# Moving operands of the fp32r matmuls read as two blocks in turn, with the storage orders set up in DRAM

## The chip, the cores and the metric

The kernel runs on one core of one Trainium2 chip. The metric is the device time of one execution in microseconds (us). Runs of this kernel agree within about 0.1%: three runs of the kernel before took 2607.55, 2608.79 and 2609.8 us.

## The reference

The input `x` is 8 batches of 3072 positions by 256 channels, in float32. Along the positions each channel is convolved with a filter given by its spectrum, and the result goes through a bilinear layer:

```
X = np.fft.rfft(x, axis=1)
F = (filt_r + 1j * filt_i)[None, :, :]
y = np.fft.irfft(X * F, n=3072, axis=1).astype(np.float32)
t = y.reshape(8 * 3072, 256)
out = ((t @ w_a) * (t @ w_b)) @ w_out          # w_a, w_b: 256 x 1536, w_out: 1536 x 256
```

## The kernel before

**The transform.** 3072 is factored as 128 x 24. A forward transform takes two steps of matmuls with tables of cosines and sines as weights: `s1` over the 128 (it takes one pair of the 24 residues at a time, 12 pairs a batch) and `s2` over the 24 (16 tiles a batch). The filter is multiplied in behind `s2` on VectorE, and the inverse goes back by `is1` (16 tiles) and `is2` (six groups `c` of four residues, in two halves `k`). Between the steps the data goes through DRAM (`zd`, `td`).

**The bilinear layer.** A visit `(c, p)` handles one group of 512 positions and one pair of 128-column blocks of `w_a` and `w_b`. It makes seven products by a 2 x 2 Strassen scheme (`product`, with the bank names x, y and z), multiplies the a part by the b part on VectorE (`parts`), splits the result into a high and a low part (`split`, on ScalarE and GpSimd), and projects it with `w_out` into the accumulators po0 and po1 (`project`). There are 36 visits a batch and 288 in all.

**The number format.** To be accurate in float32, nearly every matmul is made three times: high x high, low x high and high x low. The operands are then of the type fp32r (F32R in the code). A matmul has a stationary operand (its weights, 128 columns, loaded by one LDWEIGHTS before each matmul) and a moving operand, whose columns are streamed past the weights: 256 columns in `s1`, `product` and `project`, 512 in most of `s2` and `is1`. `is2` and the transform of batch 0 (the `first_` functions) use plain fp32 operands, except for 24 fp32r matmuls in `first_s1`.

**Which operand moves.** In `product` the moving operand is the activations `ah`/`al` (made in `is2`, 256 positions), in `project` it is a row block of `w_out` (256 output channels), in `s1` it is the input `xh`/`xl`, in `s2` the transformed data `zt`, and in `is1` the filtered spectrum `yh`/`yl` (256 channels each, one or two of them).

**What sets the order.** The order on each engine is written out by hand (`manual_schedule`). The visits are the main loop; `plan` and `early` put the steps of the next batch's transform into slots between the products of a visit: the pairs of `s1` in the first half of a batch, and one tile of `s2` and one of `is1` in each of 16 visits of the second half. SyncE (SP) issues nearly all loads, ScalarE's queue the stores of the transform.

**Names and lines.** L385 is the matmul of `s1`; L420, L422 and L423 those of `turn`, which `s2` and `is1` call (L420 for tile 0 alone); L615 that of `is2`; L646 that of `product`; L678 that of `project`; L537, L499, L501, L505 and L517 belong to batch 0's front. On VectorE, L657 is `parts`, L915, L935 and L937 add up the products, L433, L435 and L441 multiply by the filter. `filts`, `nyq` hold the filter's rows and its last row; `small_tables` issues four small loads at the start.

Of the kernel before, what the change touches and what calls it, by code (L numbers as in the profile page):

```python
# [9 lines left out]
F32 = mybir.dt.float32  # L10
# [4 lines left out]
ALU = mybir.AluOpType  # L15
# [3 lines left out]
B, S, D, DFF = 8, 3072, 256, 1536  # L19
N1, N2 = 128, 24  # L20
NB = 32
# [5 lines left out]
NJ = 16  # L27
ORDER = [(w[0], int(w[1])) for w in "a0 b0 a1 b1 o0 a2 b2 o1 o2 a3 b3 o3 a4 b4 a5 b5 o4 o5".split()]
EARLY = 11
BESIDE = {i: (11 + i, None) for i in range(7)}  # L30
ODD = [1, 5, 7, 11, 13, 17, 19, 23]

FOLDED = [0, 12] + [n for k in range(1, 12) for n in (k, 24 - k)]
WHOLE = [0, 3, 6, 9]
# [30 lines left out]
def _exact(v, n):  # L65

    if n in ODD or n % 6 == 0:
        return v
# [7 lines left out]
def _tables():  # L76
# [3 lines left out]
    g = np.zeros((N2, 128, N1))  # L80
    for n2 in range(N2):
        n = N2 * n1 + n2
        for j in range(NB):
            for s in range(2):
                k1 = 32 * s + j
                r, i = 4 * j + s, 4 * j + 2 + s
# [52 lines left out]
    order = [n for p in PAIRS for n in p]  # L139
    hi, lo = np.zeros((2, 96, 128)), np.zeros((2, 96, 128))  # L140
    bhi, blo = np.zeros((2, 128, 96)), np.zeros((2, 128, 96))
    fc = np.zeros((128, 3, 128))
    ic = np.zeros((128, 3, 96))
    fix = np.vectorize(_exact)
    for kind in range(2):
# [4 lines left out]
        for ri in range(2):  # L150
            for s in range(2):
# [3 lines left out]
                for k2 in range(N2):  # L155
                    r = 64 * ri + 24 * s + k2
                    row = inv[kind, r] * fac[k2]
                    bhi[kind, r], blo[kind, r] = _split(row if kind else fix(row, k2))
    fl = hi.transpose(1, 0, 2)
    fc.reshape(4, 32, 3, 128)[:, :24] = np.stack([hi[0], hi[1], lo[1]], 1).reshape(4, 24, 3, 128)  # L160
    ic[:, 0], ic[:, 1], ic[:, 2] = bhi[0], bhi[1], blo[1]
    sc = np.zeros((128, 2))
# [10 lines left out]

    s1c = np.stack(_split((s1 / fac[:, None, None])[order]), 1).reshape(NI, 2, 2, N1, 128).transpose(0, 3, 1, 2, 4)
    s1f = s1[[0, 12, *range(1, 12)]].transpose(1, 0, 2)
    g = g.reshape(N2, NJ, 2, 4, N1).transpose(0, 1, 3, 2, 4)
    gc = g.reshape(NC, 4, 128, N1).transpose(0, 2, 1, 3)
    ff, fi = fwd.reshape(2, 4, N2, 128)[:, :, FOLDED], np.zeros((128, 4, 96))
    ff[:, 2:, [f > 12 for f in FOLDED]] *= -1
    ff = ff.reshape(2, 96, 128).transpose(1, 0, 2)  # L180
# [25 lines left out]


@with_exitstack
def fft_filter_bilinear_kernel(ctx: ExitStack, tc, x, x0, filt, fny, wa, wb, wo, s1c, gc, fc, fl, ic, sc, s1f, ff, fi, out):
    nc = tc.nc  # L210
    f32 = lambda t: t.bitcast(F32)

    def pool(name, bufs=1, space=None):
        kw = {} if space is None else {"space": space}
# [8 lines left out]
    fr = front.enter_context(tc.tile_pool(name="fr", bufs=2, side="right"))  # L223
# [19 lines left out]
    def bank_f(shape, kind=F32, lane=0):  # L243
        if kind == F32 and not streaming:
            turns[0] += 1
        tag = f"f{lane}" if kind != F32 else "f1" if streaming else f"f{turns[0] % 2}"
        return ps_f.tile(shape, kind, name="ps", tag=tag)
# [16 lines left out]
    cut = pw.tile([128, 2], F32, name="cut")  # L264
    filts = [const.tile([128, 2, 2, D], F32, name=f"filt{i}") for i in range(2)]
    nyq = const.tile([128, D], F32, name="nyq")


    def conv_load(w, queue):
# [69 lines left out]
    for k, p in ORDER:  # L339
        if k == "o":  # L340
            conv.append([wo.bitcast(I32).rearrange("(f p) (d w) -> p f d w", p=128, w=2)[:, 2 * p:2 * p + 2], p, 2])
        else:
            w = (wa if k == "a" else wb).bitcast(I32).rearrange("(k p) (f w) -> p k f w", p=128, w=2)
# [36 lines left out]
    def s1(b, i):  # L380
        (xh, xl), st = held.pop(("xs", b, i)), held.pop(("s", b, i))
        ps = bank_f([128, 2, D])
        for n in range(2):
            for q, (w, m) in enumerate(((0, xh), (0, xl), (1, xh))):
                nc.tensor.matmul(ps[:, n], st[:, n, w], m[:, n], start=q == 0, stop=q == 2)  # L385
        zh = later[0].tile([128, 2, D], F32R, name="zh", tag="e1")
        zl = later[0].tile([128, 2, D], F32R, name="zl", tag="e2")
        nc.scalar.copy(out=zh, in_=ps)
        nc.vector.tensor_tensor(out=zl, in0=ps, in1=f32(zh), op=ALU.subtract)
        held["zs", b, i] = zh, zl  # L390
# [25 lines left out]
    def turn(i, w, wl, hi, lo, ps):  # L416

        if i == 0:
            for q, (m, v) in enumerate(((w[:, 1], hi), (wl[:, 1], lo), (w[:, 2], hi))):
                nc.tensor.matmul(ps[:, 0], m, v[:, 0], start=q == 0, stop=q == 2)  # L420
        j = 1 if i == 0 else 0
        nc.tensor.matmul(ps[:, j:2], w[:, 0], hi[:, j:2], start=True, stop=False)  # L422
        nc.tensor.matmul(ps[:, j:2], wl[:, 0], lo[:, j:2], start=False, stop=True)  # L423

    half = [slice(0, 64), slice(64, 128)]

# [93 lines left out]

    def first_f(g):
        f = [*filts, more][g % 3].rearrange("p a n d -> p (a n) d")
        nc.sync.dma_start(out=f, in_=filt[64:192, 4 * g:4 * g + 4])
        held["f0", g] = f

    def first_z(g, parts=1):
# [25 lines left out]
    def first_s2(i):  # L552
        g, h = divmod(i, 2)
        zt, f = (held[k, g][:, 2 * h:2 * h + 2] for k in ("z0", "f0"))
        bank, tag = BANKS[i % 4]
        ps = bank.tile([128, 2, D], F32, name="ps", tag=tag)
        first_turn(i, [fcf], [zt[0:96]], ps)
        y = fr.tile([128, 2, D], F32, name="y0", tag="y", bufs=4)
        v = fr.tile([128, 2, D], F32, name="v0", tag="v", bufs=4)

        nc.vector.tensor_tensor(out=y, in0=ps, in1=f, op=ALU.mult)
        if ("w", i) in held:
            nc.vector.tensor_tensor(out=v, in0=ps, in1=held.pop(("w", i)), op=ALU.mult)
        else:
            nc.vector.tensor_tensor(out=v[0:64], in0=ps[64:128], in1=f[0:64], op=ALU.mult)
            nc.vector.tensor_tensor(out=v[64:128], in0=ps[0:64], in1=f[64:128], op=ALU.mult)
        if i == 0:
            r = 64 if 0 in swapped else 0
            nc.vector.tensor_tensor(out=v[r:r + 1, 0], in0=ps[64:65, 0], in1=nyq[64:65], op=ALU.mult)
        held["y0", i] = [y, v]  # L570

    def first_is1(i):
# [37 lines left out]

    def is2(b, c, k):
        tt, gt, ah, al = held["t", b, c]
        ps = bank_f([128, 4, N1])
        for n in range(4):
            nc.tensor.matmul(ps[:, n], tt[:, n, 128 * k:128 * k + 128], gt[:, n], start=True, stop=True)  # L615
        ps = ps.rearrange("p (h n) m -> p h (n m)", h=2)
        v = nc.vector
        if k == 0:
            x0 = moe[0].tile([128, 2, 256], F32, name="x0", tag="x0")
            t = moe[0].tile([128, 4, 256], F32, name="t", tag="ot")  # L620
            held["b", b, c] = x0, t
            nc.scalar.copy(out=x0, in_=ps)
            nc.scalar.copy(out=ah[:, 0], in_=x0[:, 0])
            v.tensor_tensor(out=t[:, 0], in0=ps[:, 1], in1=x0[:, 0], op=ALU.subtract)
            v.tensor_tensor(out=al[:, 0], in0=x0[:, 0], in1=f32(ah[:, 0]), op=ALU.subtract)
            return
        x0, t = held.pop(("b", b, c))
        nc.scalar.copy(out=ah[:, 1:3], in_=ps)
        v.tensor_tensor(out=al[:, 1:3], in0=ps, in1=f32(ah[:, 1:3]), op=ALU.subtract)
        v.tensor_tensor(out=t[:, 1], in0=ps[:, 1], in1=t[:, 0], op=ALU.subtract)  # L630
        v.tensor_tensor(out=t[:, 2], in0=ps[:, 1], in1=x0[:, 1], op=ALU.subtract)
        v.tensor_tensor(out=t[:, 3], in0=ps[:, 0], in1=t[:, 1], op=ALU.subtract)
        for i in (0, 2):
            nc.scalar.copy(out=ah[:, 3 + i:5 + i], in_=t[:, i:i + 2])
            nc.gpsimd.tensor_tensor(out=al[:, 3 + i:5 + i], in0=t[:, i:i + 2], in1=f32(ah[:, 3 + i:5 + i]), op=ALU.subtract)
# [4 lines left out]
    def product(b, c, p, i, bank, first=False):  # L640
        m, n = FACTORS[i]
        _, _, ah, al = held["t", b, c]
        for k in range(2):
            wh, wl = wab[p][k]
            for q, (w, v) in enumerate(((wh, ah), (wh, al), (wl, ah))):
                nc.tensor.matmul(  # L646
                    bank[:, k], w[:, m], v[:, n], start=first and k == 0 and q == 0, stop=q == 2, skip_group_check=True
                )

# [20 lines left out]
    def project(r, f, some=range(4)):  # L670
        b, c, p = r["at"]
        gh, gl = (t.rearrange("p h (n m) -> p (h n) m", n=2) for t in r[f"f{f}"])
        if p == r["from"] and f == 0:
            po[b, c] = [ps_o.tile([128, 2, D], F32, name=f"po{i}", tag=f"po{i}") for i in range(2)]
        for n in some:
            o = po[b, c][n // 2][:, n % 2]
            for q, (g, w) in enumerate(((gh, wo_h), (gh, wo_l), (gl, wo_h))):
                nc.tensor.matmul(  # L678
                    o, g[:, n], w[p][:, 1 - f], start=p == r["from"] and f == 0 and n % 2 == 0 and q == 0,
                    stop=p == r["to"] and f == 1 and q == 2, skip_group_check=True,  # L680
                )
# [73 lines left out]
    with tc.manual_schedule():  # L755
# [29 lines left out]
        def small_tables():  # L785
            nc.sync.dma_start(out=fcf, in_=ff)
            nc.sync.dma_start(out=icf, in_=fi)
            nc.sync.dma_start(out=nyq[64:65], in_=fny)
            nc.sync.dma_start(out=sct, in_=sc)

# [54 lines left out]
        for b in range(B):  # L845
# [55 lines left out]
            for v, (c, p) in enumerate(VISITS if b == 0 else [(c, p) for c in range(NC) for p in range(NP)]):  # L901
# [3 lines left out]
                r = {"at": (b, c, p), "from": NP // 2 if halves and p >= NP // 2 else 0, "to": NP // 2 - 1 if halves and p < NP // 2 else NP - 1}  # L905
# [46 lines left out]
        one, r = prev  # L952
# [43 lines left out]
```

## Time and profile before

| what | value |
|---|---|
| median of three runs | 2608.79 us |
| the profiled execution | 2609.38 us |
| its span, first to last instruction | 2607.5 us |
| TensorE busy, matmul / weight load | 99% / 96% |
| VectorE, ScalarE, GpSimd busy | 70%, 54%, 48% |
| mean granted TensorE clock | 0.997 of full speed |
| matmuls, each with one weight load | 20934 |

How to read it: matmuls are pipelined, and the duration that the profile gives for one (about 280 ns for 256 columns) is the time from its start to its modelled end, so consecutive ones overlap. What a matmul costs in a full stream is its pitch: the difference of the start times of two neighbours. Pitches are read from the timeline, whose first column is the start in us. A line of the timeline that ends in x4 merges four equal instructions.

### The profile page before, as it was taken

To read this page: it belongs to the slowest core of one execution; us is meant where nothing else is said; L and a number is where in the kernel's file an instruction comes from. 1 tells how busy PE (TensorE), PEld (TensorE's weight loads), DVE (VectorE), ACT (ScalarE), POOL (GpSimd) and SP (SyncE) were. 2 spreads that over 40 slices of the span, in tenths; PEclk is the share of its full clock that TensorE was granted. 3 is DMA by queue.
4 is the path that set the end of the run, shared out by engine and by line. 5 is a ranking of instruction groups with operands and counts; after the bars stand their busy time and mean duration, and the time that the engine had idled before them with its cause. 6 is when DMAs were issued, how large, how long until landed. Compare 5 with 4: busy or idle time off the path is not lost.

```text
span 2607.5 us, 53389 instructions
## 1 busy us (share of the span) xinstructions
PE 2572.0 (99%) x20934; PEld 2508.2 (96%) x20934; DVE 1813.1 (70%) x2511; ACT 1409.5 (54%) x2480; POOL 1246.8 (48%) x926
## 2 busy tenths in 40 slices
PE   7899999999999999999999999999999999999999
PEld 3699999999999999999999999999999999999999
DVE  6776995569855797558965589655995569855554
ACT  5655555555555455555555555555555555544444
POOL 4664544445445454444444444444554445534333
PEclk9999999999999999999999999999999999999999
DMA  9446433344323552245413544144432444310100
GB/s 307 150 135 212 136 120 99 135 136 144 103 93 130 152 154 84 90 139 164 137 63 117 162 133 127 55 157 137 134 114 84 142 138 141 101 36 22 41 21 17
DMA packets 209421, 310.65 MB, mean 119 GB/s; under 512 B 19185, under 2 KB 119474, under 8 KB 209090
## 3 DMA queue, kind: packets, MB, share of 16 engines
q1 hardware_dynamic: 166578, 230.55, 28.6%
q10 hardware_dynamic: 42592, 76.70, 8.4%
q8 instruction: 164, 2.69, 0.4%
q14 instruction: 87, 0.71, 0.1%
HBM read 202.31 MB, written 108.45 MB: 119 GB/s over the span
## 4 chain that ended last, share of the span: by engine, by line
PE 94%; DMA 2%; POOL 1%; DVE 1%; issue 1%; ACT 1%; SPq 0%; ACTq 0%; DVEq 0%; POOLq 0%
PE x L646 31%; PE po L678 31%; PE z L646 15%; PE y L646 8%; PE ps L615 3%; PE ps L385 2%; PE ps L422 2%; PE ps L423 2%; DMA filt<-in_filt 1%; DMA z<-x 0%; PE ps L420 0%; DMA zf<-z 0%; POOL m L316 0%; DMA td<-t 0%; DMA gt<-in_gc 0%
## 5 line engine op out<-in xcount | busy, mean ns | idle before, releaser
L666 POOL TENSOR_TENSOR gl<-g,gh 128x512 fp32r<-128x512 f32 x574 | 785.4, 1370 | 898.6 <-ACT gh L665 884.7
L657 DVE TENSOR_TENSOR g<-c 128x512 f32<-128x512 f32 x576 | 598.8, 1040 | 292.1 <-ACT c L946 171.5
L678 PE MATMUL po<-woh,gh 128*128 128x256 f32 x2304 | 655.1, 284 | 2.2 <-DVE filt L685 2.2
L678 PE MATMUL po<-woh,gl 128*128 128x256 f32 x2304 | 646.6, 281 | 0.0
L678 PE MATMUL po<-wol,gh 128*128 128x256 f32 x2304 | 645.2, 280 | 0.0
L946 ACT COPY c<-x 128x512 f32<-128x512 f32 x288 | 169.0, 587 | 780.1 <-PE x L646 753.2
L678 PEld LDWEIGHTS po<-woh,gh 128*128 128x128 f32 x2304 | 434.7, 189 | 12.8 <-DVE filt L685 2.6
L678 PEld LDWEIGHTS po<-wol,gh 128*128 128x128 f32 x2304 | 434.5, 189 | 7.5
L678 PEld LDWEIGHTS po<-woh,gl 128*128 128x128 f32 x2304 | 433.9, 188 | 0.1
L665 ACT CAST gh<-g 128x512 fp32r<-128x512 f32 x576 | 357.3, 620 | 63.0 <-PE po L678 52.8
L935 DVE TENSOR_TENSOR c<-x,c 128x512 f32<-128x512 f32 x288 | 197.7, 686 | 219.0 <-PE x L646 196.2
L646 PE MATMUL x<-ah,wah 128*128 128x256 f32 x1152 | 325.5, 283 | 4.5 <-ACT c L910 3.2
L646 PE MATMUL x<-ah,wbl 128*128 128x256 f32 x1152 | 323.4, 281 | 0.0
L646 PE MATMUL x<-al,wbh 128*128 128x256 f32 x1152 | 323.1, 280 | 0.0
L646 PE MATMUL x<-al,wah 128*128 128x256 f32 x1152 | 322.9, 280 | 0.0
L646 PE MATMUL x<-ah,wbh 128*128 128x256 f32 x1152 | 322.6, 280 | 0.0
L646 PE MATMUL x<-ah,wal 128*128 128x256 f32 x1152 | 322.0, 280 | 0.0
L646 PEld LDWEIGHTS x<-ah,wah 128*128 128x128 f32 x1152 | 217.6, 189 | 5.9 <-ACT c L910 4.0
L646 PEld LDWEIGHTS x<-al,wah 128*128 128x128 f32 x1152 | 218.4, 190 | 0.0
L646 PEld LDWEIGHTS x<-ah,wal 128*128 128x128 f32 x1152 | 217.6, 189 | 0.0
L646 PEld LDWEIGHTS x<-ah,wbl 128*128 128x128 f32 x1152 | 217.0, 188 | 0.0
L646 PEld LDWEIGHTS x<-ah,wbh 128*128 128x128 f32 x1152 | 216.9, 188 | 0.0
(145 smaller groups left out, 5950.5 us busy)
## 6 DMA issues: line engine op xcount, KB each, us to landing
z<-zh ACTq DMA_DIRECT2D x112, 256.0 KB, 2.3
filt<-in_filt SPq DMA_DIRECT2D x112, 256.0 KB, 2.8
zth<-z SPq DMA_DIRECT2D x112, 256.0 KB, 3.0
tt<-td SPq DMA_DIRECT2D x94, 256.0 KB, 4.0
out<-ot SPq DMA_DIRECT2D x47, 512.0 KB, 3.0
td<-t ACTq DMA_DIRECT2D x114, 192.0 KB, 2.1
xt<-in_x SPq DMA_DIRECT2D x84, 256.0 KB, 3.5
st<-s1d SPq DMA_DIRECT2D x84, 256.0 KB, 2.7
```

The costliest lines, as they stand in the source:

```text
L385: nc.tensor.matmul(ps[:, n], st[:, n, w], m[:, n], start=q == 0, stop=q == 2)
L422: nc.tensor.matmul(ps[:, j:2], w[:, 0], hi[:, j:2], start=True, stop=False)
L423: nc.tensor.matmul(ps[:, j:2], wl[:, 0], lo[:, j:2], start=False, stop=True)
L615: nc.tensor.matmul(ps[:, n], tt[:, n, 128 * k:128 * k + 128], gt[:, n], start=True, stop=True)
L646: nc.tensor.matmul(bank[:, k], w[:, m], v[:, n], start=first and k == 0 and q == 0, stop=q == 2, skip_group_check=True)
L657: nc.vector.tensor_tensor(out=gt, in0=g[:, :, 0], in1=g[:, :, 1], op=ALU.mult)
L665: nc.scalar.copy(out=gh, in_=gt)
L666: low.tensor_tensor(out=gl, in0=gt, in1=f32(gh), op=ALU.subtract)
L678: nc.tensor.matmul(o, g[:, n], w[p][:, 1 - f], start=p == r["from"] and f == 0 and n % 2 == 0 and q == 0, stop=p == r["to"] and f == 1 and ...
L935: nc.vector.tensor_tensor(out=c1[:, 1], in0=bx, in1=c1[:, 1], op=ALU.add)
L946: nc.scalar.copy(out=c1[:, 0], in_=bx)
```

## The change

No instruction changes its place on any engine, and one small DMA on SP is added. What changes is the access pattern of the operands and the order in which data is stored:

- A helper `mm` takes the moving operand of `s1`, `product`, `project` and of tile 0 in `turn` as two blocks of 128 columns, and reads them in turn: column 0 of the first block, column 0 of the second, column 1 of the first, and so on. The output is written in one run as before. The other matmuls of `turn` do the same for 2 x 256 columns. With the pattern written as pairs of step and count, a moving operand was [1, 256] and is [1, 128] [128, 2].
- So that the output columns come out in their natural order, the stored operand has the even columns first and the odd ones behind. `_halves` makes that order. `w_out` and the filter are given to the kernel in that order (`FILTERED`), and `x` in the order that becomes natural after three such reads (`GIVEN`): `s1`, `s2` and `is1` each undo one level.
- For `product` the table `g` of `is2` has its 128 columns in that order, and `is2` writes each matmul's output as two runs of 64 columns, so that `ah`/`al` stand with the even positions first.
- Batch 0's front is not changed and keeps the natural order; it gets its own copies of the filter in DRAM (`filt0`, `fny0`) and its own tile `nyq0` of 1 KB a partition, filled by one more DMA in `small_tables`.
- The 24 fp32r matmuls of `first_s1` (L505) read one run as before.

```diff
+def _halves(order):
+    return np.asarray(order).reshape(-1, 2).T.ravel()
+FILTERED = _halves(range(D))
+TURNED = _halves(FILTERED)
+GIVEN = _halves(TURNED)
...
-    g = g.reshape(N2, NJ, 2, 4, N1).transpose(0, 1, 3, 2, 4)
+    g = g[:, :, _halves(range(N1))].reshape(N2, NJ, 2, 4, N1).transpose(0, 1, 3, 2, 4)
...
+    def mm(out, w, m, **kw):
+        out, m = out.rearrange("p (a k) -> p a k", k=2), m.rearrange("p (k a) -> p a k", k=2)
+        nc.tensor.matmul(out, w, m, **kw)
...
-                nc.tensor.matmul(ps[:, n], st[:, n, w], m[:, n], start=q == 0, stop=q == 2)
+                mm(ps[:, n], st[:, n, w], m[:, n], start=q == 0, stop=q == 2)
...
-        j = 1 if i == 0 else 0
-        nc.tensor.matmul(ps[:, j:2], w[:, 0], hi[:, j:2], start=True, stop=False)
-        nc.tensor.matmul(ps[:, j:2], wl[:, 0], lo[:, j:2], start=False, stop=True)
+                mm(ps[:, 0], m, v[:, 0], start=q == 0, stop=q == 2)
+            for q, (m, v) in enumerate(((w[:, 0], hi), (wl[:, 0], lo))):
+                mm(ps[:, 1], m, v[:, 1], start=q == 0, stop=q == 1)
+            return
+        out, hi, lo = ps.rearrange("p j (a k) -> p j a k", k=2), *(v.rearrange("p j (k a) -> p j a k", k=2) for v in (hi, lo))
+        nc.tensor.matmul(out, w[:, 0], hi, start=True, stop=False)
+        nc.tensor.matmul(out, wl[:, 0], lo, start=False, stop=True)
...
-        ps = bank_f([128, 4, N1])
+        ps = bank_f([128, 2, 256])
         for n in range(4):
-            nc.tensor.matmul(ps[:, n], tt[:, n, 128 * k:128 * k + 128], gt[:, n], start=True, stop=True)
-        ps = ps.rearrange("p (h n) m -> p h (n m)", h=2)
+            to = ps[:, n // 2].rearrange("p (k n a) -> p k n a", k=2, n=2)[:, :, n % 2]
+            nc.tensor.matmul(
+                to, tt[:, n, 128 * k:128 * k + 128], gt[:, n].rearrange("p (k a) -> p k a", k=2), start=True, stop=True
+            )
...   # product and project
-                nc.tensor.matmul(
+                mm(
...
+            nc.sync.dma_start(out=nyq0[64:65], in_=fny0)
...   # before the launch
-    filt = filt[[0, 0, 1]].reshape(192, NB, D)
-    fny = np.asarray(filt_r)[S // 2:]
+    filt0 = filt[[0, 1]].reshape(128, NB, D)
+    filt = filt[[0, 0, 1]].reshape(192, NB, D)[:, :, FILTERED]
+    fny0 = np.asarray(filt_r)[S // 2:]
+    fny = fny0[:, FILTERED]
...
-        "x": given(x), "x0": given(x0), "filt": given(filt), "fny": given(fny),
-        "wa": given(moe_w_a), "wb": given(moe_w_b), "wo": given(moe_w_out),
+        "x": given(np.asarray(x)[:, :, GIVEN]), "x0": given(x0),
+        "filt": given(filt), "fny": given(fny), "filt0": given(filt0), "fny0": given(fny0),
+        "wa": given(moe_w_a), "wb": given(moe_w_b), "wo": given(np.asarray(moe_w_out)[:, FILTERED]),
```

## Rows read from the trace of the kernel before

**Rows 1.** The page, engines: busy us (share of the span) xinstructions.

```profile
PE 2572.0 (99%) x20934; PEld 2508.2 (96%) x20934; DVE 1813.1 (70%) x2511; ACT 1409.5 (54%) x2480; POOL 1246.8 (48%) x926
```

**Rows 2.** The page, the chain that ended last, by engine.

```profile
PE 94%; DMA 2%; POOL 1%; DVE 1%; issue 1%; ACT 1%; SPq 0%; ACTq 0%; DVEq 0%; POOLq 0%
```

**Rows 3.** Windows: stretch, length, busy us of each engine, clock, DMA share, GB/s.

```profile
100.00:200.00 100.00, 92.26 (x739) 90.15 (x739) 75.89 (x111) 62.63 (x111) 65.40 (x45) 0.97 0.37 125
...
800.00:1600.00 800.00, 800.00 (x6649) 792.13 (x6649) 577.14 (x784) 435.63 (x771) 385.40 (x285) 1.00 0.41 128
```

**Rows 4.** Windows of line L646 (`product`) alone, the whole span.

```profile
0.00:2608.00 2608.00, 1525.35 (x12096) 1470.08 (x12096) 1.00 0.38 119
```

**Rows 5.** Windows of line L678 (`project`) alone, the whole span.

```profile
0.00:2608.00 2608.00, 917.58 (x6912) 869.84 (x6912) 1.00 0.38 119
```

**Rows 6.** Groups by line and shape, PE: names, shapes, count, busy us, mean ns.

```profile
L385 PE MATMUL ps<-xh,st 128*128 128x256 f32 x336 | 73.9, 282 | 0.0
L385 PE MATMUL ps<-xl,st 128*128 128x256 f32 x168 | 47.8, 285 | 1.3 <-POOL xl L377 1.3
L422 PE MATMUL ps<-yh,ict 128*96 128x512 f32 x105 | 41.7, 397 | 0.0
```

**Rows 7.** Timeline of PE: start us, duration us, then the instruction.

```profile
1001.74 0.28 PE L646 MATMUL x<-ah,wah 128*128 128x256 f32 x1
...
1005.18 0.28 PE L646 MATMUL x<-ah,wbl 128*128 128x256 f32 x1
1005.30 0.40 PE L422 MATMUL ps<-yh,ict 128*96 128x512 f32 x1
1005.53 0.39 PE L423 MATMUL ps<-yl,ict 128*96 128x512 f32 x1
1005.76 0.28 PE L678 MATMUL po<-woh,gh 128*128 128x256 f32 x1
```

**Rows 8.** Timeline of PE late in the span, where the DMA engines rest.

```profile
2530.35 0.28 PE L678 MATMUL po<-woh,gh 128*128 128x256 f32 x1
...
2534.61 0.28 PE L646 MATMUL x<-ah,wah 128*128 128x256 f32 x1
```

**Rows 9.** Timeline of PE in batch 0's front: plain fp32 operands.

```profile
37.16 0.60 PE L537 MATMUL ps<-y,icf 128*96 128x256 f32 x2
37.59 0.59 PE L537 MATMUL ps<-v,icf 128*96 128x256 f32 x2
...
56.72 1.02 PE L537 MATMUL ps<-v,icf 128*96 128x512 f32 x2
57.58 1.02 PE L537 MATMUL ps<-zf,fcf 96*128 96x512 f32 x2
```

**Rows 10.** Timeline of PE around the last `is2`.

```profile
2546.82 1.05 PE L615 MATMUL ps<-gt,tt 128*128 128x128 f32 x8
2547.62 0.37 PE L678 MATMUL po<-woh,gh 128*128 128x256 f32 x1
```

**Rows 11.** Windows with and without tiles of `s2` and `is1`.

```profile
565.00:700.00 135.00, 135.00 (x1094) 132.16 (x1093) 122.85 (x158) 74.67 (x134) 70.96 (x51) 1.00 0.39 120
700.00:865.00 165.00, 165.00 (x1402) 164.85 (x1401) 90.77 (x136) 90.02 (x158) 75.72 (x59) 1.00 0.37 121
```

**Rows 12.** Timeline of DVE over one visit with `s2` and `is1`.

```profile
599.89 1.79 DVE L657 TENSOR_TENSOR g<-c 128x512 f32<-128x512 f32 x1
...
603.09 0.69 DVE L935 TENSOR_TENSOR c<-x,c 128x512 f32<-128x512 f32 x1 [0.68 <-ACT gh L665]
...
608.58 1.79 DVE L657 TENSOR_TENSOR g<-c 128x512 f32<-128x512 f32 x1
```

**Rows 13.** Timeline of SP's queue at the start.

```profile
11.05 0.29 SPq L788 DMA_DIRECT2D nyq<-in_fny  x1
11.88 0.35 SPq L789 DMA_DIRECT2D sct<-in_sc  x1
14.23 8.21 SPq L511 DMA_DIRECT2D z<-x  x5
```

More of the change, by code (lines that the diff above doesn't have):

```diff
@@ L208, in fft_filter_bilinear_kernel @@
 @with_exitstack
-def fft_filter_bilinear_kernel(ctx: ExitStack, tc, x, x0, filt, fny, wa, wb, wo, s1c, gc, fc, fl, ic, sc, s1f, ff, fi, out):
+def fft_filter_bilinear_kernel(ctx: ExitStack, tc, x, x0, filt, fny, filt0, fny0, wa, wb, wo, s1c, gc, fc, fl, ic, sc, s1f, ff, fi, out):
     nc = tc.nc
     f32 = lambda t: t.bitcast(F32)
+    def mm(out, w, m, **kw):
+        out, m = out.rearrange("p (a k) -> p a k", k=2), m.rearrange("p (k a) -> p a k", k=2)
+        nc.tensor.matmul(out, w, m, **kw)
     def pool(name, bufs=1, space=None):
@@ L266, in fft_filter_bilinear_kernel @@
     nyq = const.tile([128, D], F32, name="nyq")
+    nyq0 = fr.tile([128, D], F32, name="nyq0", bufs=1)
     def conv_load(w, queue):
@@ L419, in turn @@
             for q, (m, v) in enumerate(((w[:, 1], hi), (wl[:, 1], lo), (w[:, 2], hi))):
-                nc.tensor.matmul(ps[:, 0], m, v[:, 0], start=q == 0, stop=q == 2)
-        j = 1 if i == 0 else 0
-        nc.tensor.matmul(ps[:, j:2], w[:, 0], hi[:, j:2], start=True, stop=False)
-        nc.tensor.matmul(ps[:, j:2], wl[:, 0], lo[:, j:2], start=False, stop=True)
+                mm(ps[:, 0], m, v[:, 0], start=q == 0, stop=q == 2)
[5 more added lines that the diff above has]
+        nc.tensor.matmul(out, wl[:, 0], lo, start=False, stop=True)
     half = [slice(0, 64), slice(64, 128)]
@@ L522, in first_f @@
         f = [*filts, more][g % 3].rearrange("p a n d -> p (a n) d")
-        nc.sync.dma_start(out=f, in_=filt[64:192, 4 * g:4 * g + 4])
+        nc.sync.dma_start(out=f, in_=filt0[:, 4 * g:4 * g + 4])
         held["f0", g] = f
@@ L568, in first_s2 @@
             r = 64 if 0 in swapped else 0
-            nc.vector.tensor_tensor(out=v[r:r + 1, 0], in0=ps[64:65, 0], in1=nyq[64:65], op=ALU.mult)
+            nc.vector.tensor_tensor(out=v[r:r + 1, 0], in0=ps[64:65, 0], in1=nyq0[64:65], op=ALU.mult)
         held["y0", i] = [y, v]
@@ L677, in project @@
             for q, (g, w) in enumerate(((gh, wo_h), (gh, wo_l), (gl, wo_h))):
-                nc.tensor.matmul(
+                mm(
                     o, g[:, n], w[p][:, 1 - f], start=p == r["from"] and f == 0 and n % 2 == 0 and q == 0,
```

## The prediction

> **What bounds the kernel now.** I read the engines' busy shares first: TensorE has 2572.0 of 2607.5 us [rows 1]. As matmuls overlap in the profile, a share of 99% does not yet say that TensorE is the bound; the chain that ended last does, with 94% on PE [rows 2]. The windows show where that holds: from 800 to 1600 us PE is busy in all of the 800 us at a clock of 1.00, while from 100 to 200 us it has 92.26 of 100 [rows 3]. So after about 200 us the time is a count of matmuls times their pitch, the distance of two starts.
>
> The pitch stands in the timeline. From 1001.74 to 1005.18 us there are 29 steps of 256 columns: 0.1186 us each [rows 7]. Late in the span, where little is loaded any more, 36 steps take 2534.61 - 2530.35 = 4.26 us: 0.1183 each [rows 8]. I use 0.1184. With 512 columns the steps are 0.23 and 0.23 [rows 7]; I use 0.2305, as starts are rounded to 0.01.
>
> The fp32r matmuls that the change touches are 12096 in `product` [rows 4], 6912 in `project` [rows 5], 336 + 168 = 504 in `s1` and four groups of 105 with 512 columns, of which one is shown [rows 6]; to these come 70 of 256 columns from tile 0 of `turn` (five in each of 14 calls, by the code). That is 19582 of 256 columns and 420 of 512. Check: 19582 x 0.1184 + 420 x 0.2305 = 2318.5 + 96.8 = 2415 us, 93% of the span, as the chain says.
>
> **Is the pitch as short as it could be?** At the granted clock, the upper level of 2.4 GHz, 256 columns at one a cycle take 106.7 ns and 512 take 213.3. The pitch is 11.7 and 17 ns longer. Plain fp32 gives a yardstick in the same trace: 256 columns take 0.43 / 2 = 0.215 us and 512 take 0.86 / 2 = 0.43 [rows 9], which is two cycles a column with almost nothing on top (213.3 and 426.7). Half of that is 107.5 and 215 ns. So at half the reading rate the stream is smooth, and at the full rate it is 7 to 10% short. Three causes can be ruled out or made unlikely by rows. It is not the weight load: there is one for a matmul of 512 columns as for one of 256, yet the excess grows from 11 to 16 ns; and eight matmuls of `is2`, each with its own load, take 0.80 us, 0.100 each [rows 10]. It is not the DMA traffic: the pitch is the same late in the span [rows 7, 8]. It is no wait for another engine: PE is never idle in these stretches [rows 3]. What is left grows with the columns and appears at the full reading rate, and that fits the reading of the moving operand, the one thing that this change alters in these matmuls.
>
> **The change part by part.**
>
> *The read of the moving operand.* No moving operand in the trace is read in two blocks, so its price is bounded from both sides. Lowest: the excess goes away, 107.5 and 215 ns by half of the plain fp32 pitch. Highest: a column taken from another place than its neighbour costs the two cycles of the plain fp32 rows, 215 and 430 ns. Between them lies 118.4, no effect. I take 110.5 ns for 256 columns and 217 for 512: the nearest row is the smooth stream, and about a quarter of the excess is kept because some of the neighbours still meet. The reason for this side: an extra of a tenth of the time cannot be a fixed price for every column, so it looks like occasional collisions of successive reads, which another order of places can lift. The sum: 19582 x (0.1184 - 0.1105) = 154.7 us, and 420 x (0.2305 - 0.217) = 5.7; together 160.4 us.
>
> The Trainium skill, "TensorE: Matmul & The Clock Gate", section "Wait — 56ns, not 53.3ns?", states a start-to-start of N / 2.4 GHz plus about 2.5 ns for a warm stream. By it the pitches would become 109.2 and 215.8 ns, the saving 180 + 6 us, and the time would be about 2423 us; the plain fp32 rows agree with it within 1 ns, and the fp32r rows of before do not.
>
> *What of it stays on the path.* In visits with one tile of `s2` and of `is1` VectorE is nearly full: 122.85 of 135 us between 565 and 700, against 90.77 of 165 in the stretch behind it [rows 11]. Such a visit takes 608.58 - 599.89 = 8.69 us [rows 12]: for TensorE 66 x 0.1184 + 4 x 0.2305 = 8.74, which is the same within rounding. In it VectorE works 0.91 x 8.69 = 7.9 us, and it waits 0.68 us once for ScalarE [rows 12]. At the new pitch TensorE would need 66 x 0.1105 + 4 x 0.217 = 8.16 us. That is just above VectorE's own work, so what is late next here is VectorE's chain with its wait. I charge 0.12 us a visit, about a quarter of the 0.55 us won; 16 visits in each of 7 batches make 112, so 14 us are lost. In the stretches without such tiles VectorE has 45% free and nothing is late. Until 200 us TensorE waits for the weights' conversion and the front (PE idle 7.7 of 100 us from 100 to 200 [rows 3]); of the gain of the 739 steps there I drop half, 3 us.
>
> *`is2`.* Its 768 matmuls now write two runs of 64 columns. No row shows a split write. Bounds: nothing, down to a gain of 3 us (0.100 us cannot fall below the cycles of the plain format by more than 4 ns), and up to a doubled pitch, 768 x 0.100 = 77 us. I take 0, since the plain format writes at half the rate and each run is long.
>
> *The added DMA.* `nyq0` is one more issue on SP, some 0.83 us (11.05 to 11.88) [rows 13]. Queued behind it are nyq, sct and the stores of z, the first at 14.23 after sct was out at 12.23: SP has 2.0 us to spare there, so the step costs 0. Without that cover it would be 0.8 us. The other loads keep sizes and rows. Work on VectorE, ScalarE and GpSimd reads the permuted tiles in one run as before: 0. The front of batch 0 is untouched.
>
> **Sum.** 160.4 - 14 - 3 = 143 us. The profiled execution took 2609.4 us, its span 2607.5 and 1.9 around it, 0.6 above the median of the runs; 2609.4 - 143 = 2466 us.
>
> **The rivals.**
>
> *Two places cost two cycles (slower).* If each column that does not stand beside the one read before it costs a read of its own, `product` and `project` go to the pitch of the plain format, 215 ns: 19582 x 0.0966 + 420 x 0.1995 = 1892 + 84 us, 4585 us. It decides as soon as the reader can hold only one place open; from 119 ns on, half a per cent over today, the kernel is slower. For it: every column now changes its place, 512 bytes away and back. Against it: nothing in the trace, as nothing is read so. The Trainium skill, "Advanced Engine Details and Errata", section "SBUF Cachelines", states that two successive hits on a 16-byte line are needed and that a different line for each access has a penalty; by that rule this rival holds, and no run here shows a case of it yet.
>
> *The gain stops at VectorE, or is half.* If VectorE's chain keeps the 112 visits at 8.69 us, 112 x 0.55 = 62 us go instead of 14, and the time is 2609.4 - (160.4 - 62 - 3) = 2514 us. If only half of the excess goes (113 ns, 223), 106 + 3 us are won and with 3 us lost at the start the time is 2503. For it: VectorE's 91% [rows 11]. Against it: part of VectorE's time there is a stretched L657 (1.79 us), which has room if it meets GpSimd less.
>
> *It does nothing.* If the excess comes from the rate and not from the places, for instance because the stream is short of bytes whatever their order, the pitch stays 118.4 ns and the time 2609 us, 2604 to 2614 with 0.2% either way. For it: the excess is nearly proportional to the columns. Against it: it is not exactly so (11 and 16).
>
> **How the numbers follow.** Forecast, 2420 to 2500 us: 0.48. Gain stopped at VectorE or half, 2500 to 2604: 0.22. Nothing: 0.09. Slower: 0.21, nearly all of it far away, by hundreds of us. A measurement here tells about 0.2%, 5 us, from no change. So faster has 0.70, the same 0.09, slower 0.21. The range from 2420 to 2612 us holds the first three cases but for their ends, some 0.78; the slower case is left out, since a range that reached to it would say nothing. The likeliest case's own range is 2420 to 2500.
>
> **What would show it.** Right: L646 and L678 at a pitch of 109 to 112 ns in the timeline, 512 columns at 216 to 219, L505 unchanged at one run, and the new waits of PE, if any, on VectorE's sums (L935, L937) in the visits with `s2`. A pitch near 215 ns shows the first rival; a pitch of 110 with PE idle in 565 to 700 shows the second; 118 the third. The prediction is wrong if the pitch moves up, or if it falls and another engine's wait takes more than 60 us.

## The result, and the profile after

The changed kernel takes 2498.43 us (median; 2497.37 to 2498.96) against 2608.92 (2607.55 to 2609.8): a ratio of 0.9576 with a 95% interval of 0.956 to 0.9593, 110 us less. Forecast were 143 us less and 2466 us; the time lies inside the range given and inside the likeliest case's own range (2420 to 2500), at its upper end.

In the changed kernel all matmuls that go through the helper stand under its line L226; L441 and L442 are `turn`, L635 is `is2`, L556 batch 0's front, L687 GpSimd's part of `split` (L666 before). First the page, its engine line and the chain:

```profile
PE 2448.1 (98%) x20934; PEld 2384.9 (96%) x20934; DVE 1799.7 (72%) x2511; ACT 1408.8 (56%) x2480; POOL 1229.5 (49%) x926
...
PE 83%; DVE 5%; POOL 4%; issue 4%; DMA 2%; ACT 2%; SPq 0%; ACTq 0%; DVEq 0%; POOLq 0%
```

The counts are those of [rows 1]; TensorE's share of the chain fell from 94 to 83% [rows 2], so other engines now stand in it now and then. The timeline of PE shows the pitch (first column: start in us):

```profile
960.24 0.38 PE L441 MATMUL ps<-yh,ict 128*96 128x512 f32 x1
960.46 0.38 PE L442 MATMUL ps<-yl,ict 128*96 128x512 f32 x1
960.67 1.05 PE L635 MATMUL ps<-gt,tt 128*128 128x128 f32 x8
...
962.90 0.28 PE L226 MATMUL x<-ah,wah 128*128 128x256 f32 x1
...
964.13 0.28 PE L226 MATMUL z<-ah,wbl 128*128 128x256 f32 x1
964.25 0.38 PE L441 MATMUL ps<-zth,fct 128*128 128x512 f32 x1
964.46 0.38 PE L442 MATMUL ps<-ztl,flt 96*128 96x512 f32 x1
964.68 0.28 PE L226 MATMUL po<-woh,gh 128*128 128x256 f32 x1
```

Eleven steps of 256 columns take 964.13 - 962.90 = 1.23 us, 0.112 each, where [rows 7] and [rows 8] had 0.118; 512 columns take 0.21 to 0.22 where they had 0.23. Over all pairs of neighbours the median pitch of 256 columns is 112 ns and its spread (5th to 95th percentile) 111 to 112; before it was 118 with 115 to 122. The stream has not only become shorter, it has become even.

The windows (stretch, length, busy us of PE, PEld, DVE, ACT, POOL, clock, DMA share, GB/s) answer to [rows 3] and [rows 11]:

```profile
100.00:200.00 100.00, 87.57 (x735) 84.59 (x734) 76.76 (x109) 62.85 (x111) 66.03 (x45) 0.98 0.38 126
...
565.00:640.00 75.00, 74.63 (x632) 73.05 (x631) 69.86 (x89) 42.24 (x76) 41.00 (x31) 1.00 0.50 156
800.00:1600.00 800.00, 798.10 (x6959) 790.35 (x6958) 609.19 (x831) 455.21 (x806) 398.76 (x299) 1.00 0.42 131
```

In 800 us stand 6959 matmuls instead of 6649. In the stretch with tiles of `s2` VectorE is busy in 69.86 of 75 us, 93%, and PE is idle in only 0.4. From 100 to 200 us PE gets no further than before (735 matmuls, 739 before) and idles 12.4 us instead of 7.7.

### The profile page after: what moved, and what is told of

It reads as the page before. It is cut to its first block, busy times and chain, and to the rows that moved or that the text cites. A ratio compares the mean times of both kernels' runs of the same rounds, so it can differ in the third digit from the quotient of the medians.

```text
span 2495.5 us, 53409 instructions
## 1 busy us (share of the span) xinstructions
PE 2448.1 (98%) x20934; PEld 2384.9 (96%) x20934; DVE 1799.7 (72%) x2511; ACT 1408.8 (56%) x2480; POOL 1229.5 (49%) x926
## 4 chain that ended last, share of the span: by engine, by line
PE 83%; DVE 5%; POOL 4%; issue 4%; DMA 2%; ACT 2%; SPq 0%; ACTq 0%; DVEq 0%; POOLq 0%
PE po L226 27%; PE x L226 27%; PE z L226 13%; PE y L226 7%; PE ps L635 3%; PE ps L226 2%; POOL gl L687 1%; PE ps L442 1%; PE ps L441 1%; POOL al L656 1%; DVE g L678 1%; POOL yl L468 1%; DMA filt<-in_filt 1%; DVE c L937 1%; DVE v L454 1%
## 5 line engine op out<-in xcount | busy, mean ns | idle before, releaser
L687 POOL TENSOR_TENSOR gl<-g,gh 128x512 fp32r<-128x512 f32 x574 | 755.1, 1318 | 819.6 <-ACT gh L686 790.9
L678 DVE TENSOR_TENSOR g<-c 128x512 f32<-128x512 f32 x576 | 541.1, 939 | 277.4 <-ACT c L968 142.8
L226 PE MATMUL po<-woh,gh 128*128 128x256 f32 x2304 | 641.4, 278 | 0.7 <-DVE filt L706 0.7
L226 PE MATMUL po<-woh,gl 128*128 128x256 f32 x2304 | 635.9, 276 | 4.5 <-POOL gl L687 3.8
L226 PE MATMUL po<-wol,gh 128*128 128x256 f32 x2304 | 633.6, 275 | 0.0
L226 PEld LDWEIGHTS po<-woh,gl 128*128 128x128 f32 x2304 | 442.2, 192 | 8.5 <-POOL gl L687 8.2
L226 PEld LDWEIGHTS po<-woh,gh 128*128 128x128 f32 x2304 | 442.3, 192 | 7.8 <-DVE filt L706 0.9
L226 PEld LDWEIGHTS po<-wol,gh 128*128 128x128 f32 x2304 | 442.3, 192 | 5.0
L226 PE MATMUL x<-ah,wah 128*128 128x256 f32 x1152 | 318.2, 276 | 9.3 <-ACT c L932 6.0
L226 PE MATMUL x<-al,wah 128*128 128x256 f32 x1152 | 317.0, 275 | 0.1
L226 PE MATMUL x<-ah,wal 128*128 128x256 f32 x1152 | 316.9, 275 | 0.0
L226 PE MATMUL x<-ah,wbh 128*128 128x256 f32 x1152 | 316.9, 275 | 0.0
L226 PE MATMUL x<-al,wbh 128*128 128x256 f32 x1152 | 316.9, 275 | 0.0
L226 PE MATMUL x<-ah,wbl 128*128 128x256 f32 x1152 | 316.9, 275 | 0.0
L226 PEld LDWEIGHTS x<-ah,wah 128*128 128x128 f32 x1152 | 221.3, 192 | 11.6 <-ACT c L932 7.1
L226 PEld LDWEIGHTS x<-al,wah 128*128 128x128 f32 x1152 | 221.3, 192 | 0.3 <-DVE al L646 0.3
L226 PEld LDWEIGHTS x<-ah,wbh 128*128 128x128 f32 x1152 | 221.3, 192 | 0.0
L226 PEld LDWEIGHTS x<-al,wbh 128*128 128x128 f32 x1152 | 221.3, 192 | 0.0
L226 PEld LDWEIGHTS x<-ah,wbl 128*128 128x128 f32 x1152 | 221.3, 192 | 0.0
```

Of the source, the lines that this page charges most:

```text
L226: nc.tensor.matmul(out, w, m, **kw)
L678: nc.vector.tensor_tensor(out=gt, in0=g[:, :, 0], in1=g[:, :, 1], op=ALU.mult)
L687: low.tensor_tensor(out=gl, in0=gt, in1=f32(gh), op=ALU.subtract)
```

## The experiments

Pitches in this part are medians of start-to-start times over all pairs in a run's trace, in ns for 256 columns, where nothing else is said; "column" is one fp32 value per partition. The three kernels that mix read orders or weights ran once each, so only their pitches are used and not their times.

**The read alone.** Two kernels part the read from the other edits. In the first, product alone reads in two blocks, and nothing is stored in another order:

```diff
-                nc.tensor.matmul(
-                    bank[:, k], w[:, m], v[:, n], start=first and k == 0 and q == 0, stop=q == 2, skip_group_check=True
+                nc.tensor.matmul(
+                    bank[:, k].rearrange("p (a k) -> p a k", k=2), w[:, m], v[:, n].rearrange("p (k a) -> p a k", k=2),
+                    start=first and k == 0 and q == 0, stop=q == 2, skip_group_check=True
                 )
```

> The kernel before with the read in two blocks of 128 in product alone; storage, is2, project, s1, s2 and is1 as before, so positions are mixed. If the read order alone makes the gain: L646 at 111.7 ns, L678 still at 118, and 12096 x 6.3 ns = 77 us less, 2532 us, less some us of new waits (2530 to 2540). If part of the gain came from the storage orders, the split write of is2 or the other edits: less than 60 us.

Measured: 2544.26 us, ratio 0.9753 (0.9725 to 0.9782), 64 us less. The timeline has the two pitches side by side: eleven steps of `project` (L679) take 1.31 us, 0.119 each, and then six of `product` 0.112 each (0.67 us).

```profile
1501.51 0.28 PE L679 MATMUL po<-woh,gh 128*128 128x256 f32 x1
...
1502.82 0.28 PE L679 MATMUL po<-woh,gl 128*128 128x256 f32 x1
1502.94 0.27 PE L646 MATMUL x<-ah,wah 128*128 128x256 f32 x1
...
1503.61 0.28 PE L646 MATMUL z<-ah,wah 128*128 128x256 f32 x1
```

The pitch is as expected; of the 77 us some 13 are not there, more than the few allowed for. By the trace, 7 of them went in `project`, which still reads in one run: its mean step rose from 119.2 to 120.3 ns. The second kernel keeps all other edits and reads in one run:

```diff
-        out, m = out.rearrange("p (a k) -> p a k", k=2), m.rearrange("p (k a) -> p a k", k=2)
         nc.tensor.matmul(out, w, m, **kw)
...
-        out, hi, lo = ps.rearrange("p j (a k) -> p j a k", k=2), *(v.rearrange("p j (k a) -> p j a k", k=2) for v in (hi, lo))
+        out = ps
```

> The kernel after with everything but the read: the storage orders, the split write of is2, the separate filter of batch 0 and the added DMA stay, and every moving operand is read in one run as before (so channels and positions come out in another order). If the read alone makes the gain: 2607 to 2611 us, with all pitches at 118 and 230. If the storage or the split write has a share, it lies off 2609 by that share.

Measured: 2610.15 us against 2610.28, ratio 0.9999 (0.9989 to 1.0009), pitch 118 again. So the whole gain is the read; the storage orders, the split write of `is2` (112 ns before and after) and the added DMA cost nothing that can be seen.

**Which orders are fast.** One kernel tries eleven orders side by side, one for each p in `product` and in `project`:

```diff
+                two = lambda a: (o.rearrange("p (b a k) -> p b a k", a=a, k=2), w, i.rearrange("p (b k a) -> p b a k", a=a, k=2))
+                if p == 0:
+                    nc.tensor.matmul(o, w, i, **kw)
+                elif p == 1:
+                    nc.tensor.matmul(*two(2), **kw)
...   # p = 2 to 5: two(4), two(16), two(64), two(128); in project:
+                turn = lambda k: (o.rearrange("p (a k) -> p a k", k=k), g1, i.rearrange("p (k a) -> p a k", k=k))
+                some_ = lambda j: (o.rearrange("p (a k j) -> p a k j", k=2, j=j), g1, i.rearrange("p (k a j) -> p a k j", k=2, j=j))
...   # p = 1 to 4: turn(4), turn(16), some_(2), some_(4)
+                elif p == 5:
+                    nc.tensor.matmul(o.rearrange("p (k a) -> p k a", k=2), g1, i.rearrange("p (a k) -> p k a", k=2), **kw)
```

> The kernel before, with another read order of the moving operand in each of the six p: product reads one run (p=0), or pairs from two blocks of 2, 4, 16, 64 and 128 columns in turn (p=1 to 5); project reads one run (p=0), 4 and 16 blocks in turn (p=1, 2), two blocks taken two and four columns at a time (p=3, 4), and every second column first (p=5). Storage is not reordered, so positions and channels come out in another order. Theory A (successive reads from one neighbourhood collide; far places lift it): 118 ns for one run and for blocks of 2, about 112 for blocks of 16 to 128, 112 for 4 and 16 blocks in turn, between the two for two and four columns at a time, 118 for every second column. Theory B (only a distance of 512 bytes matters): 112 for blocks of 128 alone, 118 for all other orders. Theory C (any order that is not one run is read in another way): 112 for all but p=0.

Its timeline (L650 one run, L652 blocks of 2, L656 blocks of 16, L698 four blocks, L700 sixteen, L702 two blocks two columns at a time, L706 every second column):

```profile
1506.52 0.28 PE L650 MATMUL x<-ah,wah 128*128 128x256 f32 x1
...
1509.26 0.28 PE L650 MATMUL x<-ah,wbl 128*128 128x256 f32 x1
...
1515.82 0.28 PE L652 MATMUL x<-ah,wah 128*128 128x256 f32 x1
...
1518.56 0.28 PE L652 MATMUL x<-ah,wbl 128*128 128x256 f32 x1
...
1533.50 0.28 PE L656 MATMUL x<-ah,wah 128*128 128x256 f32 x1
...
1536.07 0.28 PE L656 MATMUL x<-ah,wbl 128*128 128x256 f32 x1
...
1531.13 0.30 PE L698 MATMUL po<-woh,gh 128*128 128x256 f32 x1
...
1532.69 0.31 PE L698 MATMUL po<-woh,gl 128*128 128x256 f32 x1
...
1539.90 0.39 PE L700 MATMUL po<-woh,gh 128*128 128x256 f32 x1
...
1542.31 0.40 PE L700 MATMUL po<-woh,gl 128*128 128x256 f32 x1
...
1501.12 0.34 PE L702 MATMUL po<-wol,gh 128*128 128x256 f32 x1
...
1502.81 0.34 PE L702 MATMUL po<-woh,gl 128*128 128x256 f32 x1
...
1512.55 0.41 PE L706 MATMUL po<-wol,gh 128*128 128x256 f32 x1
...
1514.86 0.41 PE L706 MATMUL po<-woh,gl 128*128 128x256 f32 x1
```

The pairs of L650, L652 and L656 are 23 steps apart: 2.74, 2.74 and 2.57 us, 119, 119 and 112 ns. L698 and L700 have 11 steps of 142 and 219, L702 and L706 ten of 169 and 231. All orders together, with those of the next kernel:

| order of the moving operand | pitch, ns |
|---|---|
| one run | 118 to 120 |
| two blocks of 2 columns in turn | 118 |
| two blocks of 4, 16, 64 or 128 columns in turn | 112 |
| two blocks of 128, 896 columns apart; each column twice in a row | 112 |
| two blocks, four columns at a time | 127 |
| two blocks, two columns at a time | 168 |
| four, eight, sixteen blocks in turn | 140, 220, 220 |
| every second column | 230 |

All three theories fell. B is wrong, since blocks of 4 columns do as well as 128; C is wrong, since many other orders are slower than one run; A is wrong in its orders with more than two blocks, which should have been as good and are far worse. What fits all of them is a description by two streams: take the reads at even places of the sequence as one stream, those at odd places as another, and let a line be four neighbouring columns. Where each stream reads four times in a row from one line, the pitch is 112; with two reads in a row (one run; blocks of 2; four at a time) it is 118 to 127; with one (all the others) 140 to 230. A kernel was made to test it:

```diff
+                if q == 0:
+                    nc.tensor.matmul(*turn(2, 128), **kw)
+                elif p == 0:
+                    nc.tensor.matmul(o.rearrange("p (a k) -> p a k", k=2), w, i[:, 0:128].unsqueeze(2).to_broadcast([128, 128, 2]), **kw)
...   # p = 1 to 4: turn(2, 126), turn(2, 127), turn(2, 125), turn(8, 32); p = 5: blocks at 0 and 896
```

> The kernel after, with another order of the moving operand in two of the three matmuls of each product, by p: every column of 128 read twice in a row (p=0), two blocks of 126, 127 and 125 columns in turn (p=1, 2, 3), eight blocks of 32 in turn (p=4), two blocks 896 columns apart (p=5). Positions are mixed and some columns left out. Theory E (odd and even reads are two streams, each of which wants four reads in a row from one line of four columns): 111.7 ns or a little less (109 where the next load allows it) for p=0 and p=5; also for 125 to 127 (scaled by the columns, and set by the weight load anyway), as each stream still reads on in its own block; far more for eight blocks, between the 140 of four and the 220 of sixteen. Theory F (two neighbouring reads must lie in different lines): p=0 is slow, 118 or more, since both reads of a pair are the same column; p=5 is 111.7.

Its timeline, L675 being the order with each column twice (L673, two blocks, stands between), and L683 the eight blocks:

```profile
1489.76 0.28 PE L675 MATMUL x<-al,wbh 128*128 128x256 f32 x1
1489.87 0.28 PE L675 MATMUL x<-ah,wbl 128*128 128x256 f32 x1
...
1490.10 0.28 PE L675 MATMUL z<-al,wah 128*128 128x256 f32 x1
1490.21 0.28 PE L675 MATMUL z<-ah,wal 128*128 128x256 f32 x1
...
1516.12 0.38 PE L683 MATMUL x<-al,wah 128*128 128x256 f32 x1
1516.32 0.40 PE L683 MATMUL x<-ah,wal 128*128 128x256 f32 x1
```

Reading every column twice in a row takes 112 (four steps in 0.45 us): neighbouring reads need not lie in different lines, so F is out and E stands. Blocks that start at another place in a line (125 to 127 columns) are as good: the three matmuls of a product, two of which have only 250, 252 or 254 columns, take 335 ns together, 3 x 111.7. Eight blocks are at the upper end of what E had allowed: the first of the two takes 204, the second 222, and the one in two blocks behind them 128 instead of 112, 552 in all, so some 220 each.

**What sets the 112.** The pitch had stopped short of the 107.5 that half of the plain fp32 pitch gives, and the weights were suspected.

```diff
+                part = 128 if q == 0 else 96 if p in (2, 4) else 64
+                if p == 0 or p >= 2 and q == 0:
+                    nc.tensor.matmul(o2, w, i2, **kw)
+                elif p == 1:
+                    nc.tensor.matmul(o2, wh_l[:, 0:256:2], i2, **kw)
+                elif p in (2, 3):
+                    nc.tensor.matmul(o2[0:part], w[:, 0:part], i2, **kw)
+                else:
+                    nc.tensor.matmul(o[0:part], w[:, 0:part], i, **kw)
...   # project: weights flat[:, n % 2:256:2] for p = 1, flat[:, n:512:4] for p = 2
```

> The kernel after, with other weights by p. Product: 128 columns in one run (p=0), 128 columns with a step of two (p=1), in two of three matmuls 96 (p=2) or 64 (p=3) columns, and the same with the moving operand read in one run again (p=4: 96, p=5: 64). Project: one run, but a step of two (p=1) and of four (p=2). Part of the sums is left out and positions are mixed. Theory A (after the change the weight load sets the pitch of 111.7 ns): two blocks with 96 or 64 weight columns fall to 109 ns, and one run stays at 117 to 118 whatever the weights. Theory D (the excess of the kernel before came from the weight load's reads meeting those of the moving operand): with 64 weight columns one run falls well below 118, by about half of the excess or 5 ns. A step in the weights: no effect if the load only counts columns (111.7), longer if its reads suffer like those of the moving operand.

In two blocks, matmuls with 96 or 64 weight columns have a mean pitch of 109.2, undisturbed pairs alone, and those with 128 have 111.6. In one run the narrower weights do not help (117 to 123): theory D is out, and the excess of the kernel before did not come from the weights. Theory A holds in the main: 128 weight columns need some 112 ns to load, which is longer than the 109.2 of the matmul in front, beside which the load runs. By the starts on record it is a matmul's own weights that count: the short pitch belongs to the one with the narrow weights, whether 96, 64 or 128 columns are loaded next.

With 128 weight columns, too, the pitch is 109 where the matmul in front leaves more time: in 77 fp32r matmuls of the changed kernel right behind one of 512 columns in `is1`, and in the 29 of `is2` that stand there, where the others have 112. In the same kernel 512 columns take 215.9 with `ict` (96 weight columns) and 218.3 with `fct` (128), whose weights are loaded beside a matmul of 256 columns; behind a matmul in one run with narrow weights, `fct` takes 215 to 216 as well. Fewer moving columns do not help either: at one column a cycle 250 columns take 2.5 ns less than 256, but in this stretch of the kernel with the blocks of 125 columns, where 16 of 24 steps have 250, all take 2.68 us, 0.1117 each:

```profile
1508.07 0.28 PE L673 MATMUL x<-ah,wah 128*128 128x256 f32 x1
1508.18 0.27 PE L681 MATMUL x<-al,wah 128*128 128x250 f32 x1
...
1510.75 0.28 PE L226 MATMUL po<-woh,gh 128*128 128x256 f32 x1
```

One matmul does not fit: 512 columns with `flt` (weights of 96 rows and 128 columns) take 220.0, though their weights have 218 ns to load. A step in the weights does cost: 120 with a step of two, and 236 with a step of four, as in this timeline of `project` (11 steps in 2.59 us):

```profile
1528.23 0.40 PE L716 MATMUL po<-woh,gh 128*128 128x256 f32 x1
...
1530.82 0.40 PE L716 MATMUL po<-woh,gl 128*128 128x256 f32 x1
```

**The new waits.** In the steady part of the changed kernel PE stops three times a batch for GpSimd's low part `gl`:

```profile
918.06 0.27 PE L226 MATMUL po<-woh,gh 128*128 128x256 f32 x1
918.17 0.28 PE L226 MATMUL po<-wol,gh 128*128 128x256 f32 x1
918.72 0.38 PE L226 MATMUL po<-woh,gl 128*128 128x256 f32 x1 [0.27 <-POOL gl L687]
```

0.55 us lie between the last two starts instead of 0.11. A kernel takes the low part last:

```diff
-        for n in some:
-            o = po[b, c][n // 2][:, n % 2]
-            for q, (g, w) in enumerate(((gh, wo_h), (gh, wo_l), (gl, wo_h))):
+        for q, (g, w) in enumerate(((gh, wo_h), (gh, wo_l), (gl, wo_h))):
+            for n in some:
+                o = po[b, c][n // 2][:, n % 2]
```

> The kernel after, with the twelve matmuls of project in another order: the eight with the high part gh first, the four with the low part gl last. If the new waits of PE for gl (22 of about 0.4 us before the first matmul with gl, GpSimd's split) are what was lost in the steady part, they go and the time falls by 6 to 9 us to about 2490. If PE only waits for the next thing behind it, or if VectorE is full there, nothing changes: 2498 within 2.

Measured: 2494.77 us (2490.79 to 2498.28), ratio to before 0.9557 (0.9536 to 0.9577). It was run once more beside the changed kernel:

> The order of project with the low part last once more, beside the changed kernel. If the waits for gl that went are a gain, it is 3 to 6 us faster than the changed kernel; if they only moved, within 2 us of it.

> The changed kernel once more, beside the next one on the same chip: 2498 us within 3.

Measured: 2494.43 us (2491.6 to 2497.17), ratio 0.956 (0.9547 to 0.9573), beside 2497.94 (2495.77 to 2501.1), ratio 0.9579 (0.9566 to 0.9592). The median is 3.7 us lower than that of the changed kernel's first series, and 3.5 us lower than that of the one beside it; but the runs and the intervals overlap, so that this version beats the changed kernel is likely and not settled by the times alone. It has no more than half of the 6 to 9 us that the waits were worth, and the lists of waits of TensorE's weight loads, from 400 us on, show where the rest went. The changed kernel, and then this one:

```profile
PEld po L226 <- POOL gl L687: 6.8, 17, 0.5
```

```profile
PEld po L226 <- DVE ot L714: 1.8, 6, 0.3
```

The 17 waits for `gl` are gone, but six new ones stand in their place: with all matmuls with `gh` first, the second accumulator of a new group is written by the third matmul and not by the seventh, and VectorE has not yet copied out what the accumulators held (`ot`). By the pitches from 380 us on, PE stops for 8.4 us in `project` in the changed kernel, and in this one still for about 4.6 us, 3.2 of them in these six places.

## Why the prediction was right, step by step

**The bound and the mechanism.** TensorE's pitch set the time, the excess of the pitch lay in the read of the moving operand, and the new order lifted it. That held: the read alone undone gives 2610 us, and the read alone in `product` gives 64 us. The reason given for it did not hold as it stood. "Another order of places can lift" collisions is true of two blocks and false of four, eight or sixteen, which are slower than one run; the forecast had the right sign by a reason too wide.

**The size of the pitch term.** It was taken as 160.4 us, with 118.4 to 110.5 and 230.5 to 217. Measured over the trace it is 118.0 to 111.7 and about 232.0 to 217.5: 19582 x 6.3 ns = 123 us and 420 x 14.5 = 6 us, 129 together. Of the 31 us too many, 8 lie in reading 118.4 off starts rounded to 10 ns, and 23 in the kept share of the excess: over the 106.7 of one column a cycle 5.0 ns stay, half of them the wait for 128 weight columns, not the 3.8 of the forecast. The forecast had ruled the weight load out. That was right for the excess of the kernel before and wrong for what lies under it: with a load of 128 columns for each matmul, 110.5 could not be reached. A row for it was there: eight matmuls of `is2` [rows 10], read as an average of 100 ns that shows a weight load at less than 107; but the last of the eight steps, to the matmul of `project` behind them, is 31 ns (the next one makes up for it with 203), and the seven others stand at 109 to 112.

**VectorE.** The step charged 14 us for VectorE's chain in 112 visits, a quarter of the gain there. The place was right and the engine wrong: VectorE follows at 93%, and PE is stopped by GpSimd's `gl` three times a batch, in 18 places behind 380 us of 0.36 to 0.54 us (8.4 us by the pitches). At the stop shown above GpSimd had been busy without a break since 912.7 us, with two `al`, one `yl` and two `gl`.

**The start.** 3 us were charged until 200 us; the 2400th matmul starts at 373.0 us instead of 380.0, where some 2000 pitches of 6.3 ns would have won 13, so it is about 6 us, up to 380 us. There other engines set the time, and a faster TensorE only waits longer: 12.4 us idle from 100 to 200 instead of 7.7 [rows 3], about half of it behind ScalarE's copies of the products (six waits, 6.0 us, where the kernel before had four of 3.2). From there on the gain grows evenly, 105 us over 18533 matmuls, 5.7 ns each.

**The sum.** 129 - 8 - 6 = 115 us against 112 of span measured; the rest is within the rounding of these terms (0.1 ns of pitch is 2 us).

**`is2`, the DMA, the storage.** Costed at 0, and the kernel with all of it but the read shows 0 within 0.1%.

**The rivals.** "Two places cost two cycles" did not happen, yet its mechanism and its price exist: sixteen blocks or every second column cost 220 to 230 ns. The Trainium skill, "Advanced Engine Details and Errata", section "SBUF Cachelines", asks for two successive hits on a 16-byte line; by that rule one run, with four, would have been free and two blocks, with one, would have paid. The trace has it the other way round, 118 against 112, and the measurement decides; counted for even and odd reads apart, the rule's direction comes back, with four hits needed and not two. The Trainium skill, "TensorE: Matmul & The Clock Gate", section "Wait — 56ns, not 53.3ns?", gives 109.2 ns for 256 columns: measured with 64 and 96 weight columns, and with 128 only where the matmul in front leaves them more than 112 ns to load.

## What to carry to other kernels

Read the pitch of back-to-back matmuls from their starts and set it beside the columns over the granted clock: an excess that grows with the columns points at the read of the moving operand, and one that does not at the weights. For fp32r a moving operand read from two blocks in turn, each block in one run, streams at 109 ns for 256 columns, 2.5 above one column a cycle, while more blocks or pairs of columns make it slower than one run; the load of 128 weight columns, 112 ns, is then the next limit; the outputs keep their order if the storage is permuted once outside. A faster TensorE gives nothing back where others already set the time, here the first 200 us, so a forecast counts only matmuls that run back to back.

## What was not expected of the hardware

- Reading a column twice in a row costs no more than reading two blocks (112), and blocks as short as 4 columns are enough.
- The order matters by a factor of two: 112 to 230 ns for the same 256 columns. Why four blocks (140) are better than two blocks two at a time (168), when by the two streams both have one read in a row, stays open.
- A load of 128 weight columns takes longer (112 ns) than 256 moving columns (109), so it sets the pitch once the read is mended. Why 512 columns with `flt` take 220.0, 4 more than with `ict`, was not found.
- Weights read with a step of two cost 120, with a step of four 236.
